# Spills queued later, weight splits ahead of the next group's words, and a group fetched sooner, in a retention and feed-forward kernel

## The chip, the cores and the metric

The kernel runs on one core of one Trainium2 chip. The metric is the device time of one execution in microseconds (us). Smaller is better.

## What is computed

The reference, cut to what matters: a retention attention (B=8, H=8, S=576, D=64), whose output is laid out as 4608 tokens of 512, and a feed-forward layer with h - tanh(h) between two products.

```python
gamma = 1.0 - 2.0 ** (-5.0 - np.arange(H))
Dmat = np.where(rel >= 0, gamma[:, None, None] ** rel, 0.0)   # rel = row - column
ret = (scale * q @ k.transpose(0, 1, 3, 2)) * Dmat @ v
x = ret.transpose(0, 2, 1, 3).reshape(B * S, H * D)           # 4608 x 512
h = x @ w_in                                                  # 512 x 2048
out = (h - np.tanh(h)) @ w_out                                # 2048 x 512
```

## The kernel before

The sequence is cut into nine chunks of 64 positions (NC); one chunk holds 512 tokens (8 batches of 64). Retention runs chunk by chunk with a state, two batches in a turn. [...]

Chunks 0 to 2 go through the feed-forward layer plainly. From chunk 3 on two chunks are taken together, and the products are made with fewer multiplications by sums of quarter blocks (seven products in place of eight). `stage_a` makes the first layer of a pair of chunks, `stage_b` (L1519) the second layer of one chunk, and in its loop over the 16 slices f the attention of the next pair: `attend` (L961) is called for every even f. `stage_b` runs for chunks 2 and 4 with attention. From chunk 5 on there are two calls of `stage_c` (L1251), for chunks 5 and 6 and for chunks 7 and 8. Each has eight passes p, and a pass makes seven products k of the first layer, 0 to 6. The results g go to HBM (`spill`). The second layer of chunks 5 to 8 comes last, as 56 products q of `second_product` (L1458): eight groups (chunk and half) of seven. Each product q needs 8 sets of two matmuls against one of seven weight variants, in the order B11, T1, T2, B22, T3, B21, T4.

The order of the work is written out by hand. `in_order` (L72) ties every engine's instructions to the order in which they are written, SP's DMA issues too. A DMA issue that waits therefore holds all issues behind it on SP, and an instruction that waits on ScalarE or VectorE holds all behind it.

What the change touches:

- `attend` has two branches, for the first and the second chunk of a pair. Both copy the attention's output with ScalarE, put words into the operands of the next products (`put`: high word on ScalarE, low word on VectorE), call `between()`, which is the split of slice f+2 of g (`split`, L1034, a cast on ScalarE at L1042, a low word on VectorE at L1043), and `prep_turn(m + 1, 1)`, which is `scale_v` (L297): four ScalarE instructions (L301), one for each of four heads, on the v of the next turn. In the second branch VectorE forms t3, t1, t2, t4 (L990 to L993) between them, and `put(3, ...)` and `put(2, ...)` need t3 and t1.
- `out_sums` (L1135) forms sums and words of w_out in chunk 4's `stage_b` and elsewhere (VectorE L1153, ScalarE L1156).
- In `stage_c`, `away` (L1287) lets GpSimd subtract the tanh from c22, c12 and c21 (L1288), and SP spills the result (L1289); g11 is made by VectorE and spilled at L1327. In the second call (chunks 7 and 8), `ahead_c` (L1398) is called after each product: it loads weight variants (`load_second`, L1339, at L1351 from `ofull` and at L1354 from `ovar`) by the table `ahead_at` (L1388), splits weights (`split_second`, L1360) and fetches groups (`fetch_group`, L1372). A load waits until the products that read its place are done.
- `fetch_group(k)` fetches the even slices (ge) and the odd slices (go) of group k, 1 MB each (L1385). The second group's are in places that hold weights of `stage_c` (xh0 and xh1).
- `split_second` makes the low word of the weight tile cast in the call before (VectorE L1364), and casts the next tile (ScalarE L1367). Each tile is a quarter of a variant. The last call but one falls on q = 3, the last on q = 4, with the low word of the last quarter of B21.
- `side(q + 3)` makes the words of product q+3: a cast on ScalarE (L1432), a low word on VectorE (L1436), and for the first three products of a group sums of g's quarters (L1434, L1442). The call for a group's first product (slices of ge alone) ends with a sum that needs ge and go. `second_product` copies some results out of PSUM on ScalarE (L1487) and adds others on VectorE (L1492, L1493).

The main loop of the second layer (L1595 on):

```python
for q in range(7 * len(GROUPS)):
    if q + 3 < 7 * len(GROUPS):
        side(q + 3)
    if 0 < q < 5:
        split_second()
    second_product(q)
```

Of the kernel before, what the change touches and what calls it, by code (L numbers as in the profile page):

```python
# [92 lines left out]
def retention_ffn(ctx: ExitStack, tc: tile.TileContext, ins, out, spill, wvar, ovar, ofull):  # L93
    nc = tc.nc
# [636 lines left out]
    for k, (n, f) in enumerate(seq):  # L731
# [12 lines left out]
        elif k in early:  # L744
            p = early[k]
# [160 lines left out]
    def prep_turn(m, t):  # L906
        if m >= len(turns) or (m, t) in prepared:
            return
        if (m, t) == (held, 1) and (m, t) not in came:
            return  # L910
        prepared.add((m, t))
        (scale_q, scale_v)[t](turns[m])
# [12 lines left out]
    def put(v, b, src, sub):  # L925

        hi, lo = [x[:, :, b * C : (b + 2) * C].rearrange("p i (u t) -> p u i t", u=2) for x in xv[v]]
        if sub == 0:
            nc.scalar.copy(hi, src)
        else:  # L930
            nc.vector.tensor_tensor(lo, src, hi.bitcast(F32), op=ALU.subtract)
# [29 lines left out]
    def attend(m, between):  # L961

        j = turns[m]
        c, b = divmod(j, B)
        first, apart = (c - FIRST) % 2 == 0, moved(j)
        if first and b == 0:
            new_xv()
        o, new = stretch(m)
        if first:
            a = pool.tile([P, 2, 4, C], F32, tag="cv", bufs=4, name=f"xa{j}")  # L970
            kept[b] = a
            put(0, b, o[:, :, 0:2], 0)
            put(5, b, o[:, :, 2:4], 0)
            nc.scalar.copy(a, o)
            prep_turn(m + 1, 1)
            between()
            put(0, b, a[:, :, 0:2], 1)
            put(5, b, a[:, :, 2:4], 1)
        else:
            a = kept.pop(b)  # L980
            t13 = pool.tile([P, 2, 2, 2, C], F32, tag="cv", bufs=4, name=f"t13_{j}")
            t24 = pool.tile([P, 2, 2, 2, C], F32, tag="cv", bufs=4, name=f"t24_{j}")
            t1, t3, t2, t4 = t13[:, 0], t13[:, 1], t24[:, 0], t24[:, 1]
            own = pool.tile([P, 2, 4, C], F32, tag="cv", bufs=4, name=f"xb{j}")
            nc.scalar.copy(own[:, :, apart:], o[:, :, apart:])
            if apart:
                nc.scalar.copy(own[:, :, :apart], new[:, :, :apart])
            put(4, b, o[:, :, 2:4], 0)
            prep_turn(m + 1, 1)
            nc.vector.tensor_tensor(t3, own[:, :, 2:4], own[:, :, 0:2], op=ALU.subtract)  # L990
            nc.vector.tensor_tensor(t1, own[:, :, 0:2], a[:, :, 0:2], op=ALU.subtract)
            nc.vector.tensor_tensor(t2, t3, a[:, :, 0:2], op=ALU.add)
            nc.vector.tensor_tensor(t4, a[:, :, 2:4], t2, op=ALU.subtract)  # L993
            put(3, b, t3, 0)
            put(2, b, t1, 0)
            between()
            put(1, b, t2, 0)
            put(6, b, t4, 0)
            put(2, b, t1, 1)
            put(1, b, t2, 1)  # L1000
            put(3, b, t3, 1)
            put(4, b, own[:, :, 2:4], 1)
            put(6, b, t4, 1)
# [238 lines left out]
    def renew(na, v):  # L1242
# [5 lines left out]
        nc.scalar.copy(xh, sources[v])  # L1248
        return lambda: nc.vector.tensor_tensor(xl, sources[v], xh.bitcast(F32), op=ALU.subtract)

    def stage_c(na, m0, lows):  # L1251

        nb, last_ = na + 1, na + 2 == NC
        if not last_:
            new_sources(na)
        for p in range(NPAIR):
            j = NPAIR - 1 - p if last_ else p
            homes_ = (("o0", "own")[p % 2], "new", "h", "h") if last_ else (("o0", "h")[p % 2], "o1", "o2", "o3")
            sums_of = None if last_ else attend_c(m0 + j)
            if sums_of and j == NPAIR - 1:  # L1260
                sums_of()
                sums_of = None
            u2, u4 = [pool.tile([P, BLK], F32, tag=t, name=f"u{t}{na}_{j}") for t in ("gh", "gl")]
            x, y, z, v = [
                psp.tile([P, BLK], F32, tag=t, bufs=2 if t == "h" else 1, name=f"p{w}{na}_{j}")
                for w, t in zip("xyzv", homes_)
            ]
            f1, f2 = 2 * j, 2 * j + 1
            c22, c12 = [pool.tile([P, BLK], F32, tag="g", bufs=3, name=f"c{t}_{na}_{j}") for t in (22, 12)]
            c21 = pool.tile([P, BLK], F32, tag="gl", name=f"c21_{na}_{j}")  # L1270

            def done(k):
                if last_:
                    ahead_c(p, k)
                elif j == NPAIR - 1 and k < 6:
                    lows.append(renew(na, k))

            def low():
                if lows:
                    lows.pop(0)()  # L1280

            def tanh(c):
                th = pool.tile([P, BLK], F32, tag="cv", bufs=4, name=f"th{na}_{j}")
                nc.scalar.activation(th, c, AF.Tanh)  # L1284
                return th

            def away(n, c, f):  # L1287
                nc.gpsimd.tensor_tensor(c, c, tanh(c), op=ALU.subtract)  # L1288
                nc.sync.dma_start(spill[n, f], c)  # L1289

            product_c(na, j, 0, x)
            nc.scalar.copy(u2, x)
            if last_ and p == 0:
                lows.append(renew(na - 2, 6))
            done(0)
            if not last_:
                load_turn(m0 + j + 3, 0)
            product_c(na, j, 1, y)
            nc.vector.tensor_tensor(u2, y, u2, op=ALU.add)
            low()  # L1300
            done(1)
            if not last_:
                load_turn(m0 + j + 2, 1)
                load_raws(6 + j)
            product_c(na, j, 2, z)
            nc.vector.tensor_tensor(u4, z, u2, op=ALU.add)
            if not last_:
                prep_turn(m0 + j + 2, 0)
            if sums_of:
                sums_of()  # L1310
            low()
            done(2)
            product_c(na, j, 3, v)
            nc.vector.tensor_tensor(c22, v, u4, op=ALU.add)  # L1314
            low()
            done(3)
            y = psp.tile([P, BLK], F32, tag=homes_[1], bufs=1, name=f"pw{na}_{j}")
            product_c(na, j, 4, y)
            load_sums(na, j - 2 if last_ else j + 2)
            away(nb, c22, f2)  # L1320
            nc.vector.tensor_tensor(c12, y, u4, op=ALU.add)  # L1321
            done(4)
            product_c(na, j, 5, x, False)
            away(nb, c12, f1)
            g11 = tanh(x)
            nc.vector.tensor_tensor(g11, x, g11, op=ALU.subtract)  # L1326
            nc.sync.dma_start(spill[na, f1], g11)  # L1327
            if not last_:
                prep_turn(m0 + j + 1, 1)
            done(5)  # L1330
            product_c(na, j, 6, v, False)
            nc.vector.tensor_tensor(c21, v, u2, op=ALU.add)
            away(na, c21, f2)
            low()
            done(6)

    second_w = {}

# [30 lines left out]

    group_g = {}  # L1370

    def fetch_group(k):  # L1372

        if k >= len(GROUPS):
            return
        n, h = GROUPS[k]
        group_g[k] = []
        for e in range(2):
            if (k % 2, e) == (0, 0):
                g = const.tile([P, NPAIR, 2 * P], F32, tag="state", name=f"ge{k}")  # L1380
            else:
                tag = {(0, 1): "xl0", (1, 0): "xh0", (1, 1): "xh1"}[k % 2, e]
                g = pool.tile([P, NPAIR, 2 * P], F32, tag=tag, bufs=1, name=f"g{'eo'[e]}{k}")
            src = spill[n].rearrange("(j e) p t -> e p j t", e=2)[e]
            nc.sync.dma_start(g, src[:, :, h * 2 * P : (h + 1) * 2 * P])  # L1385
            group_g[k].append(g)

    ahead_at = {  # L1388
        (0, 0): [(T1, 0), (T1, 1)], (0, 4): [(T1, 2), (T1, 3)], (1, 0): [(B11, 0)], (2, 0): [(B11, 1), (B11, 2)],
# [8 lines left out]
    def ahead_c(p, k):  # L1398

        for at, i in ahead_at.get((p, k), []):  # L1400
            load_second(at, i)
        if (p, k) == (3, 6):
            fetch_group(0)
        if (p, k) == (7, 6):
            fetch_group(1)
            for i in range(4):
                load_second(T4, i)
        if (p, k) in SPLITS:
            split_second()
        if (p, k) in ((5, 5), (6, 2), (7, 0), (7, 2), (7, 3), (7, 4), (7, 5)):  # L1410
            next(pieces)
# [181 lines left out]
    for n in range(LATE, NC, 2):  # L1593
        stage_c(n, 8 * (n - FIRST) // 2 + 8 if n < NC - 2 else None, lows)
    for q in range(7 * len(GROUPS)):  # L1595
        if q + 3 < 7 * len(GROUPS):
            side(q + 3)
        if 0 < q < 5:
            split_second()
        second_product(q)  # L1600
    in_order(tc)


# [71 lines left out]
```

## Time and profile before

| | |
|---|---|
| median of three runs | 845.14 us (844.36 to 847.79) |
| the profiled execution | 844.95 us, of which the span is 843.0 us |
| TensorE busy | 824.9 us, 98% of the span |
| VectorE busy | 598.0 us, 71% |
| ScalarE busy | 409.3 us, 49% |
| GpSimd busy | 97.9 us, 12% |
| mean granted TensorE clock | 0.994 of full speed |
| HBM traffic | 241 GB/s over the span |

The profile is of one execution. PE is TensorE, DVE VectorE, ACT ScalarE, POOL GpSimd, SP the engine that issues nearly all DMAs; a name with a q behind it (SPq) is the engine's queue. L with a number is a line of the kernel. A row of a timeline gives the start in us, the duration, the engine and line, the operation, what is written and read, and in brackets how long the engine was idle before it and what released it. [...]

### The profile page before, as it was taken

Reading aid. Unit: us, or ns where it says so; the run is one execution under the profiler, and the core shown is the slowest. Engines: PE = TensorE matmul, PEld = TensorE weight load, DVE = VectorE, ACT = ScalarE, POOL = GpSimd, SP = SyncE. Lnnn points to the kernel's source line nnn. Section 1 sums busy time; section 2 is a strip of 40 time slices with the busy share of each in tenths; the row PEclk is TensorE's granted clock in tenths of the full one; section 3 lists DMA queues with packets and bytes.
Section 4 is the critical chain, followed back from the end, with each engine's and each line's share of the span. In section 5 each row is a group of like instructions: output and inputs, shape, how many; then the busy total and the mean of one; then the engine's idle time right before and its main releaser. Section 6 shows DMA issues by size and latency. Waiting matters only on the chain. (4 is left out here: it accounts for less than half of the span.)

```text
span 843.0 us, 19242 instructions
## 1 busy us (share of the span) xinstructions
PE 824.9 (98%) x7829; PEld 687.3 (82%) x7830; DVE 598.0 (71%) x947; ACT 409.3 (49%) x772; POOL 97.9 (12%) x79
## 2 busy tenths in 40 slices
PE   7999999999999999999999999999999979999997
PEld 6888888888888888888888788788888868888886
DVE  6999877777567675666657765456855868888884
ACT  4987755544335452423345644244644544454542
POOL 0000001010000001212110003233334410000000
PEclk9999999999999999999999999999999998999999
DMA  9967968885777668576658989785489897444411
GB/s 353 365 239 264 359 212 259 243 264 192 230 274 271 202 238 300 201 279 243 238 149 302 329 298 352 278 292 200 171 290 326 322 323 243 134 126 125 125 32 43
DMA packets 94519, 204.10 MB, mean 242 GB/s; under 512 B 9184, under 2 KB 35168, under 8 KB 90976
## 3 DMA queue, kind: packets, MB, share of 16 engines
q1 hardware_dynamic: 93984, 202.10, 70.3%
q8 instruction: 61, 1.00, 0.5%
q10 hardware_dynamic: 448, 0.79, 0.2%
q14 instruction: 26, 0.21, 0.1%
HBM read 135.22 MB, written 67.63 MB: 241 GB/s over the span
## 5 line engine op out<-in xcount | busy, mean ns | idle before, releaser
L1473 PE MATMUL b<-w,s 128*128 128x512 f32 x336 | 118.9, 401 | 5.3 <-DVE w L1364 4.8
L572 PE MATMUL o<-wo,gh 128*128 128x512 f32 x432 | 111.0, 394 | 1.7 <-issue 1.0
L514 PE MATMUL h<-xh,wi 128*128 128x512 f32 x380 | 96.5, 392 | 0.3 <-ACT wi L148 0.3
L572 PEld LDWEIGHTS o<-wo,gh 128*128 128x128 f32 x432 | 79.8, 188 | 19.8 <-issue 1.2
L1477 PE MATMUL b<-w,s 128*128 128x256 f32 x336 | 87.4, 281 | 0.0
L1288 POOL TENSOR_TENSOR c<-c,th 128x512 f32<-128x512 f32 x48 | 63.7, 1331 | 189.8 <-ACT th L1284 176.9
L514 PEld LDWEIGHTS h<-xh,wi 128*128 128x128 f32 x380 | 70.5, 188 | 15.8 <-ACT wi L148 0.7
L1473 PEld LDWEIGHTS b<-w,s 128*128 128x128 f32 x336 | 62.0, 191 | 17.4 <-DVE w L1364 5.1
L1284 ACT ACTIVATE th<-c 128x512 f32<-128x512 f32 x48 | 30.1, 632 | 83.2 <-DVE c L1314 59.5
L1477 PEld LDWEIGHTS b<-w,s 128*128 128x128 f32 x336 | 64.2, 191 | 3.8
L572 PE MATMUL o<-wo,gl 128*128 128x512 f32 x216 | 59.7, 389 | 0.0
L344 PE MATMUL own<-qk,state 64*64 64x64 f32 x888 | 55.3, 221 | 0.0
L344 PE MATMUL own<-qk,vr 64*64 64x64 f32 x888 | 54.1, 220 | 0.0
L514 PE MATMUL h<-xl,wi 128*128 128x512 f32 x192 | 51.7, 390 | 0.0
L572 PEld LDWEIGHTS o<-wo,gl 128*128 128x128 f32 x216 | 40.5, 188 | 8.5
L344 PEld LDWEIGHTS own<-qk,vr 64*64 64x64 f32 x888 | 44.5, 135 | 0.0
L344 PEld LDWEIGHTS own<-qk,state 64*64 64x64 f32 x888 | 44.5, 134 | 0.0
L1085 POOL TENSOR_TENSOR c<-c,th 128x512 f32<-128x512 f32 x16 | 20.9, 1324 | 192.7 <-ACT th L1081 192.7
L1201 PE MATMUL px<-xhv,raw 128*128 128x512 f32 x128 | 40.8, 398 | 1.8 <-issue 1.8
L514 PEld LDWEIGHTS h<-xl,wi 128*128 128x128 f32 x192 | 36.0, 188 | 7.6
L301 ACT ACTIVATE vr<-vr,vtab 128x128 f32<-128x128 f32 x100 | 32.0, 395 | 11.8 <-DMA vr<-in_qkv_dram 11.8
L344 PEld LDWEIGHTS s<-qk 64*64 64x64 f32 x928 | 29.6, 134 | 9.4 <-issue 5.3
(331 smaller groups left out, 1910.8 us busy)
## 6 DMA issues: line engine op xcount, KB each, us to landing
spill_dram<-c SPq DMA_DIRECT2D x64, 256.0 KB, 3.7
s<-spill_dram SPq DMA_DIRECT2D x62, 256.0 KB, 3.9
qk<-in_qkv_dram SPq DMA_DIRECT2D x29, 512.0 KB, 5.0
vr<-in_qkv_dram SPq DMA_DIRECT2D x29, 512.0 KB, 4.9
wt<-wvar_dram SPq DMA_DIRECT2D x14, 1024.0 KB, 7.5
ws<-wvar_dram SPq DMA_DIRECT2D x13, 1024.0 KB, 5.4
spill_dram<-g SPq DMA_DIRECT2D x36, 256.0 KB, 3.3
rwi<-in_w_in_dram SPq DMA_DIRECT2D x16, 512.0 KB, 6.0
```

What stands on the lines that cost most here:

```text
L301: nc.scalar.activation(v[:, :, i], v[:, :, i], AF.Copy, scale=vtab[:, n, i : i + 1])
L344: nc.tensor.matmul(out_, w, x, start=start, stop=stop)
L514: nc.tensor.matmul(hp, win[f][:, cc // 2, a, cc % 2 * P : (cc % 2 + 1) * P], x[:, cc, :], start=(k == 0), stop=(k == 3 * NCC - 1))
L572: nc.tensor.matmul(ops[n][t], g[:, t * P : (t + 1) * P], wout[f_][:, a, :], start=(f_ == first and k == 0), stop=(f_ == final and k == 2),)
L1085: nc.gpsimd.tensor_tensor(c, c, tanh(c), op=ALU.subtract)
L1201: nc.tensor.matmul(into, w[:, a, k], x[:, k], start=start and i == 0, stop=i == len(terms) - 1, skip_group_check=not start,)
L1284: nc.scalar.activation(th, c, AF.Tanh)
L1288: nc.gpsimd.tensor_tensor(c, c, tanh(c), op=ALU.subtract)
L1473: nc.tensor.matmul(to, hi[:, j], ws, start=fresh and j == 0, stop=last_, skip_group_check=not fresh)
L1477: nc.tensor.matmul(to[:, 0], lo[:, j], ws[:, 0], start=False, stop=False, skip_group_check=not fresh)
```

## The change

Four edits.

1. In `attend`, `prep_turn(m + 1, 1)` is written behind `between()`: v is scaled behind the split of g.
2. In `stage_c`, spills are put on a list and written into SP's order two products later, behind the loads of `ahead_c` at that place; the rest of the list follows at the end of the stage.
3. The second group's go is fetched after product 1 of the last pass and its ge after product 5, in place of both after product 6.
4. In the main loop, `split_second` comes ahead of `side(q + 3)`, and for q = 0 the product comes ahead of `side(3)`.

```diff
@@ attend, first branch
             nc.scalar.copy(a, o)
+            between()
             prep_turn(m + 1, 1)
-            between()
@@ attend, second branch
             put(4, b, o[:, :, 2:4], 0)
-            prep_turn(m + 1, 1)
             nc.vector.tensor_tensor(t3, own[:, :, 2:4], own[:, :, 0:2], op=ALU.subtract)
...
             put(3, b, t3, 0)
             put(2, b, t1, 0)
             between()
+            prep_turn(m + 1, 1)
             put(1, b, t2, 0)
@@ stage_c
+    to_spill = []
+    def spill_made(wait):
+        while to_spill and to_spill[0][0] <= made_at[0] - wait:
+            _, n, f, c = to_spill.pop(0)
+            nc.sync.dma_start(spill[n, f], c)
+    made_at = [0]
...
             def done(k):
+                made_at[0] += 1
                 if last_:
                     ahead_c(p, k)
                 elif j == NPAIR - 1 and k < 6:
                     lows.append(renew(na, k))
+                spill_made(2)
...
                 nc.gpsimd.tensor_tensor(c, c, tanh(c), op=ALU.subtract)
-                nc.sync.dma_start(spill[n, f], c)
+                to_spill.append((made_at[0], n, f, c))
...
-            nc.sync.dma_start(spill[na, f1], g11)
+            to_spill.append((made_at[0], na, f1, g11))
...
             done(6)
+        spill_made(0)
@@ fetch_group, ahead_c
-    def fetch_group(k):
+    def fetch_group(k, parts=(0, 1)):
...
-        for e in range(2):
+        for e in parts:
...
+        if (p, k) == (7, 1):
+            fetch_group(1, (1,))
+        if (p, k) == (7, 5):
+            fetch_group(1, (0,))
         if (p, k) == (7, 6):
-            fetch_group(1)
             for i in range(4):
                 load_second(T4, i)
@@ main loop
     for q in range(7 * len(GROUPS)):
+        if 0 < q < 5:
+            split_second()
+        if q == 0:
+            second_product(q)
         if q + 3 < 7 * len(GROUPS):
             side(q + 3)
-        if 0 < q < 5:
-            split_second()
-        second_product(q)
+        if q:
+            second_product(q)
```

## Rows read from the trace of the kernel before

**Rows 1.** TensorE's waits in the span: us in total, times, longest.
```profile
PE b L1473 <- DVE w L1364: 4.8, 1, 4.8
PE px L1201 <- issue: 1.8, 1, 1.8
PE b L1473 <- ACT u L1487: 0.5, 1, 0.5
```

**Rows 2.** One window of 1 us: busy times by engine, clock, DMA share, GB/s.
```profile
699.00:700.00 1.00, 1.00 (x5) 0.90 (x4) 1.00 (x1) 0.00 (x0) 0.00 (x0) 0.50 1.09 348
```

**Rows 3.** The chain that ended last: start, us, what.
```profile
680.98 12.77 DMA go<-spill_dram
693.78 1.23 DVE sums L1442
```

**Rows 4.** TensorE's timeline: the first matmuls of products 0, 8 and 12.
```profile
673.70 0.39 PE L1473 MATMUL b<-w,s0vr 128*128 128x512 f32 x1
...
703.98 0.39 PE L1473 MATMUL b<-w,s8vr 128*128 128x512 f32 x1
...
715.16 0.39 PE L1473 MATMUL b<-w,s12vr 128*128 128x512 f32 x1
```

**Rows 5.** ScalarE's timeline at the start of the second phase.
```profile
678.41 1.03 ACT L1432 CAST s<-sums 128x1024 fp32r<-128x1024 f32 x1
679.35 0.57 ACT L1487 COPY u<-b 128x512 f32<-128x512 f32 x1
...
681.29 0.59 ACT L1487 COPY p<-b 128x512 f32<-128x512 f32 x1
```

**Rows 6.** VectorE's timeline: a split of w_out and half a total.
```profile
685.95 0.69 DVE L1364 TENSOR_TENSOR w<-w 128x512 fp32r<-128x512 f32 x1
686.55 0.68 DVE L1492 TENSOR_TENSOR t<-b,u 128x512 f32<-128x512 f32 x1
```

**Rows 7.** SP's timeline at the end of the last pass.
```profile
668.77 0.32 SPq L1289 DMA_DIRECT2D spill_dram<-c  x1
...
683.12 6.15 SPq L1354 DMA_DIRECT2D w<-ovar_dram  x4
```

**Rows 8.** Windows of 4 us, with the columns of rows 2.
```profile
670.00:674.00 4.00, 4.00 (x20) 3.30 (x19) 4.00 (x5) 2.19 (x4) 1.49 (x1) 1.00 0.71 227
...
682.00:686.00 4.00, 4.00 (x25) 3.46 (x24) 3.75 (x6) 3.30 (x5) 0.00 (x0) 1.00 0.98 324
686.00:690.00 4.00, 4.00 (x25) 3.50 (x24) 1.66 (x4) 0.00 (x0) 0.00 (x0) 1.00 1.09 370
```

**Rows 9.** DMA issues at 683.1 us: T4's first quarter, KB, us to landing.
```profile
w<-ovar_dram SPq DMA_DIRECT2D x1, 512.0 KB, 11.9
```

**Rows 10.** Timeline in chunk 4's `stage_b`, a turn of the first branch.
```profile
443.20 1.29 ACT L301 ACTIVATE vr<-vr,vtab 128x128 f32<-128x128 f32 x4
...
445.12 0.25 PE L344 MATMUL own<-qk,vr 64*64 64x64 f32 x2
```

**Rows 11.** Timeline there, a turn of the second branch, and TensorE's next wait.
```profile
465.96 1.28 ACT L301 ACTIVATE vr<-vr,vtab 128x128 f32<-128x128 f32 x4
...
468.20 0.74 ACT L929 CAST xhv<-t 128x256 fp32r<-128x256 f32 x2 [0.96 <-DVE t L990]
468.23 0.23 PE L344 MATMUL own<-qk,vr 64*64 64x64 f32 x2
...
468.85 0.61 ACT L1042 CAST gs<-s 128x512 fp32r<-128x512 f32 x1
...
474.87 0.98 PE L572 MATMUL o<-wo,gh 128*128 128x512 f32 x3 [0.65 <-DMA vr<-in_qkv_dram]
```

**Rows 12.** Windows of 1 us, TensorE alone: busy time, clock, DMA share, GB/s.
```profile
527.00:528.00 1.00, 0.00 (x0) 1.00 1.02 385
...
530.00:531.00 1.00, 1.00 (x4) 0.50 0.99 346
...
532.00:533.00 1.00, 1.00 (x4) 0.53 1.01 377
```

## What the change does to the time: a prediction

> **What bounds the kernel now.** I read the page's table of busy times first: TensorE is busy 98% of the span (the table above), so only its idle time and its clock can give anything back. The list of TensorE's waits then names the places: 4.8 us once on VectorE's L1364, 0.5 us on a ScalarE copy at L1487, and 1.8 us on something the profile doesn't show [rows 1]. The first two lie in the second phase (the products q of L1458, from 673 us on). [...] The chain that ended last tells why L1364 was late: the second half of the second group was issued at 680.98 us and took 12.77 us to land, and only then could VectorE do a sum of that group (L1442, 1.23 us) [rows 3]. VectorE works in the written order, and the last low word of w_out is written behind that sum.
>
> **The stall in the second phase.** Its price is read from TensorE's timeline. Product 0 starts at 673.70 us, product 8 at 703.98, product 12 at 715.16 [rows 4]. Four undisturbed products take 11.18 us, 2.795 each; eight would take 22.36 and took 30.28. So 7.9 us are lost in the first eight: 4.8 and 0.5 of waits, and some 2.6 us of the low clock and of starting up. I take all 7.9 as removable and go through what could be late next, with product q starting at 673.70 + 2.795 q.
>
> Product 0 ahead of the words of product 3. ScalarE's copy of product 0 stood behind the cast of those words: the cast at 678.41 us, the copy at 679.35, the copy of product 1 at 681.29 [rows 5]. Changing places, the copy starts at 678.4 and ends at 679.0, before product 2 wants the bank at 679.3: the 0.5 us goes. The cast starts at 678.9, and VectorE's low word for product 3 at 679.95; it ends at 681.2, product 3 starts at 682.1. The copy of product 1 still ends at 681.9, only 0.2 us before product 3 needs its bank; between nothing and 0.3 us may remain, and I take nothing, since the copies keep their sum.
>
> The last low word. Split ahead of the words of q+3, it comes behind the total of product 3 on VectorE: from 679.95 us four low words of s (1.2 us each, as the sum of the same shape [rows 3]), three splits (0.7) and a total (0.7 and a half-width 0.4) [rows 6], and ends at 688.7 us. Product 5 wants it for its last quarter, at 687.7 + 2.1 = 689.8 us. It fits by 1.1 us.
>
> The spills and the second group. SP issues in order and stood behind GpSimd's products: the last spill of the group before at 668.77 us, the second group at 680.98, T4 behind it from 683.12 [rows 3, 7]. The 668.77 us spill still waits for its GpSimd product in the same place, so the change starts there: go at about 669.1, B21's last loads by 671, T3 by 673.4 (two of its homes are read until product 5 of that pass, about 672.4), ge at 673.5, T4 by 676 or as the queue lets it. Behind them come the c spills, and behind those only later fetches. In bytes from 669.1 to T4's end: c 0.26 MB, go 1.05, B21 0.52, T3 2.10, ge 1.05, c 0.26, T4 2.10, together 7.34 MB. At 324 GB/s, what a full queue moved at 682 to 686 us, that is 22.7 us, to 691.8; at 370 GB/s (686 to 690 us) 19.8 us, to 688.9 [rows 8]. Product 6 reads T4's first quarter at 690.5 and its last at 692.6 us; the first quarter lies 1.57 MB ahead, at 684.6 to 687. T3 is there by 681.2 (wanted 684.9), ge by 684.5 (its cast comes at about 685.2). So T4's last quarter has 0.8 to 3.7 us to spare. Before, it landed 11.9 us after its issue [rows 9], later than that, and nobody waited, since TensorE itself was late.
>
> The words of the second group then follow on VectorE by the same durations: low word 7 at 689.9, its sum 691.1, total of product 4, t1, low word 8 at 694.6 (wanted 696.1), its sum, total of product 5, low word 9 at 698.1 (wanted 698.9), low word 10, after its cast of 1.05, at 701.6 (wanted 701.7). These are tight, but instructions of VectorE overlap a little, which I left out. In the stage with the first four groups' spills the deferral moves no load in SP's order, and TensorE waits there only the unnamed 1.8 us; nothing is gained or lost.
>
> **v scaled behind g's split.** This edit moves four ScalarE instructions of each turn (1.28 us together) behind a cast, and in every second turn also behind two casts that wait for VectorE's t3 and t1. I went through all turns: in most, v is still waiting for its load at that point, or TensorE comes 1 us or more later. The closest harmless one is at 443.20 us: a cast (0.52 us) put ahead gives heads at 444.1 to 445.0, and the next attention reads its first v at 445.12 [rows 10]. One turn isn't harmless. There VectorE is behind with the sums of w_out, and t3 comes late. Before, v was scaled from 465.96 us without it, and the attention read its first v at 468.23 [rows 11]. After, ScalarE must first do the casts of t3 and t1 (468.20) and of g (468.85); v's heads come from 469.4 on, the first ready at 469.8, the last at 470.7. TensorE stops for 1.6 us, and then some 0.06 us at each of three heads: 1.8 us. That delay covers the 0.65 us for which TensorE waited, to 474.87 us, on a load issued before the stop [rows 11]; 1.15 us stay. The clock: the nearest row is the unnamed 1.8 us wait at 527 us, beside an attention of the same kind, after which the clock was 0.50 to 0.53 from 530 to 533 us, three windows that lost 1.5 us together [rows 12]. Here a stop of about that length comes just ahead of the attention. The bounds are 0 and 1.5 us; I take 1.5, by that nearest row. What the edit gives (g's words sooner) is nothing, since TensorE never waited for g there.
>
> The sum against the profiled execution's own 844.95 us (0.2 below the median of 845.14): 844.95 - 7.9 + 1.8 - 0.65 + 1.5 = **839.7 us**.
>
> **Rivals.**
> First, v's delay costs less: no clock is lost (838.2), or the stop is covered too (837.0). For it: the stop is somewhat shorter than the wait at 527 us. Against: nothing on ScalarE's written order lets v pass the casts.
>
> Second, something of the second group is late: T4's landing, or VectorE's words 8 to 10. A ring that gives no more than 300 GB/s lands T4 24.5 us after 669.1, at 693.6: a stop of 1 us, and with late words and the clock up to 4. That gives 840.7 to 843.7.
>
> Third, the one that ends slower: T4 is now queued behind both halves of the group. If the queue moves 227 GB/s, as at 670 to 674 us when little was asked of it [rows 8], the 7.34 MB take 32.3 us and T4's last quarter lands at 701.4; TensorE stops in product 6 for 9 us and loses 2 us of clock: 850.7. It is slower than before from where stop and clock exceed 5.3 us, below some 270 GB/s. Against it: both stretches with a full queue [rows 8]. [...]
>
> Fourth, the change doesn't do what it says: go's home is free later than I think, it is issued as late as before, and only the low word moves. Then product 7 waits for its words instead of product 5; some 3 of the 7.9 us are saved: 844.6.
>
> **How the numbers follow.** The forecast, with clock losses from 1 to 2 us (839.2 to 840.2, and 0.6 either way for other executions), has 0.42; the first rival 0.26, the second 0.20, the third 0.07, the fourth 0.05. The range takes in the first rival down to 836.4 and the second up to 843.5. What a measurement can tell from no change is about 0.5%, 4.2 us: faster means below 840.9. That is all of the first rival, 0.34 of the forecast and little of the second: 0.62. Slower is the third, 0.06 of its 0.07. The rest, 0.32, is the same.
>
> **What would show it.** Right: product 8 starts 7.9 us sooner relative to product 0, no wait on L1364, a clock of 1.00 at that place, go issued about 12 us sooner; in the stage with attention a new TensorE wait on L301 of 1.6 to 2 us near 468 us, the 0.65 us gone, a clock of 0.50 for 2 to 3 us behind it. Wrong: TensorE waiting in products 6 to 10 for a load of w or for L1436, no wait on L301, or the unnamed 1.8 us gone or elsewhere, which would move the time by up to 3 us either way.

## The result, and the profile after

Median after: 839.14 us (836.91 to 839.77), against 845.58 (844.36 to 848.54) for the kernel before beside it; the ratio is 0.9914 [0.9892, 0.9936], that is 6.4 us or 0.9% faster. The forecast was 839.7 in a range of 836.4 to 843.5. The time came out; its terms did so only in part, and the runs below show which.

The profiled execution of after took 839.53 us, its span is 837.7 us, TensorE is busy 823.9 us of it and the mean granted clock is 1.00 (0.994 before). The lines have moved: the products' matmuls are now L1489 and L1493, their copies L1503, the casts and low words of g L1448 and L1452, its sums L1458, the split of w_out L1377, the fetch L1398, the loads L1364 and L1367.

TensorE's waits after (as rows 1: us in total, times, longest):

```profile
PE px L1201 <- issue: 2.0, 1, 2.0
PE o L572 <- issue: 1.3, 1, 1.3
...
PE o L572 <- DMA vr<-in_qkv_dram: 0.9, 2, 0.5
PE s L344 <- DVE qk L295: 0.4, 1, 0.4
PE own L344 <- ACT vr L301: 0.4, 1, 0.4
```

The 4.8 us on the low word of w_out (a tile less its cast) [rows 1] is gone and no load has come in its place. The wait on the scaling of v is there (last line); it is the first part of a longer stop, 0.4 us where the prediction had 1.6. The two "issue" waits, which name no cause, were there before too (1.8 and 1.0 us).

The second phase after, TensorE's timeline (as rows 4), one window of 1 us (as rows 2), and SP's timeline (as rows 7):

```profile
675.90 0.39 PE L1489 MATMUL b<-w,s0vr 128*128 128x512 f32 x1
...
698.76 0.40 PE L1489 MATMUL b<-w,s8vr 128*128 128x512 f32 x1
...
709.94 0.40 PE L1489 MATMUL b<-w,s12vr 128*128 128x512 f32 x1
```

```profile
699.00:700.00 1.00, 1.00 (x8) 0.91 (x7) 1.00 (x1) 0.55 (x1) 0.00 (x0) 1.00 0.49 154
```

```profile
671.86 0.43 SPq L1398 DMA_DIRECT2D go<-spill_dram  x1
...
675.78 0.43 SPq L1398 DMA_DIRECT2D ge<-spill_dram  x1
677.36 0.32 SPq L1257 DMA_DIRECT2D spill_dram<-c  x1
678.10 4.36 SPq L1367 DMA_DIRECT2D w<-ovar_dram  x4
```

Products 0 to 7 take 22.86 us in place of the 30.28 of before [rows 4]: 7.42 us gained, 0.5 from the best that was forecast (22.36). The clock at 699 us is 1.00, not 0.50 [rows 2]. go is issued 4.0 us before product 0 starts (671.86 against 675.90), where it used to be issued 7.3 us after (680.98 against 673.70 [rows 3, 4]): 11.3 us sooner. T4's issue begins 2.2 us after the start of product 0 instead of 9.4 [rows 7].

Where the two traces part, as the drift of TensorE's timeline against before (the start of the same attention or product, after minus before). The second execution profiled is the same kernel, run again later (d2 below):

| stretch | after | after, again |
|---|---|---|
| start to 240 us (no edited line runs) | +0.56 | +0.04 |
| 240 to 437 us (chunks 0 to 3) | -0.01 | +0.04 |
| 437 to 512 us (chunk 4 with attention) | +2.46 | -0.25 |
| 512 to 551 us (the unnamed wait and its clock) | -1.31 | +0.20 |
| 551 us to product 0 | +0.50 | +0.15 |
| products 0 to 7 | -7.42 | -7.40 |
| rest | 0.0 | 0.0 |
| sum, the difference of the spans | -5.2 | -7.2 |

So the second phase is the same to 0.02 us, and what differs between two executions of one kernel, 2 us here, lies ahead of it. That is what makes edit 1 hard to price, and seven of the experiments bear on its price.

### The profile page after: what moved, and what is told of

Its sections match the earlier page's. It is cut to its first block, busy times and chain, and to the rows that moved or that the text cites. A ratio compares the mean times of both kernels' runs of the same rounds, so it can differ in the third digit from the quotient of the medians.

```text
span 837.7 us, 19247 instructions
## 1 busy us (share of the span) xinstructions
PE 823.9 (98%) x7830; PEld 685.0 (82%) x7830; DVE 598.6 (71%) x947; ACT 409.7 (49%) x772; POOL 98.0 (12%) x79
## 5 line engine op out<-in xcount | busy, mean ns | idle before, releaser
L1489 PE MATMUL b<-w,s 128*128 128x512 f32 x336 | 117.5, 397 | 0.1
L1493 PE MATMUL b<-w,s 128*128 128x256 f32 x336 | 87.0, 279 | 0.0
L1489 PEld LDWEIGHTS b<-w,s 128*128 128x128 f32 x336 | 61.2, 188 | 12.1 <-ACT u L1503 0.4
L1493 PEld LDWEIGHTS b<-w,s 128*128 128x128 f32 x336 | 63.4, 189 | 3.7
L301 ACT ACTIVATE vr<-vr,vtab 128x128 f32<-128x128 f32 x100 | 31.9, 394 | 7.6 <-DMA vr<-in_qkv_dram 7.6
```

The lines of the kernel that those rows point to most:

```text
L301: nc.scalar.activation(v[:, :, i], v[:, :, i], AF.Copy, scale=vtab[:, n, i : i + 1])
L1489: nc.tensor.matmul(to, hi[:, j], ws, start=fresh and j == 0, stop=last_, skip_group_check=not fresh)
L1493: nc.tensor.matmul(to[:, 0], lo[:, j], ws[:, 0], start=False, stop=False, skip_group_check=not fresh)
```

## The experiments

The table gives for each kernel the median, the ratio to the kernel before, and from its profile the time from product 0 to product 8 and the drift from 437 to 512 us against before. The second to fourth columns hold "old" where an edit is undone.

| kernel | v (edit 1) | spills (2), fetch (3) | order (4) | median us | ratio | products 0 to 7 | 437 to 512 |
|---|---|---|---|---|---|---|---|
| before | old | old, old | old | 845.58 | 1 | 30.28 | 0 |
| after | new | new, new | new | 839.14 | 0.9914 [0.9892, 0.9936] | 22.86 | +2.46 |
| x1 | old | new, new | new | 838.94 | 0.9907 [0.9882, 0.9933] | 22.87 | -1.08 |
| x2 | new | old, old | old | 845.79 | 0.9994 [0.9977, 1.001] | 29.47 | +0.13 |
| x3 | old | old, old | new | 844.64 | 0.997 [0.9952, 0.9988] | 28.85 | +0.52 |
| x4 | old | new, new | old | 838.59 | 0.9907 [0.988, 0.9933] | 23.74 | +0.58 |
| x5 | old | old, new | new | 842.71 | 0.9954 [0.9937, 0.997] | 25.51 | -1.10 |
| x6 | old in one turn | new, new | new | 836.83 | 0.9891 [0.9869, 0.9914] | 22.87 | +0.57 |
| x7 | old | new, old | new | 839.26 | 0.9914 [0.9885, 0.9943] | 24.16 | +2.32 |
| x8 | new in first branch | new, new | new | 838.91 | 0.992 [0.9889, 0.9952] | 22.85 | +0.79 |
| d1 | as x6 | new, new | new | 837.92 | 0.9888 [0.9864, 0.9912] | 22.86 | -0.61 |
| d2 | new | new, new | new | 838.22 | 0.9895 [0.987, 0.9919] | 22.88 | -0.25 |
| d3 | as x1 | new, new | new | 841.1 | 0.9914 [0.9887, 0.9941] | 22.83 | +1.29 |
| d4 | later still in one turn | new, new | new | 839.06 | 0.9904 [0.9878, 0.9931] | 22.63 | +1.03 |

The kernel before had medians of 846.24 beside x1 to x4, 846.1 beside x5 to x8 and 847.4 beside d1 to d4.

### Which edit frees the second phase: x2, x3, x4, x5, x7

**x2, edit 1 alone.** The only edit to the kernel before is the diff of `attend`.

> The kernel before with the move of v behind g's split alone. Theory: 1 to 2.4 us slower than before (845.6): 846.6 to 848.0, with a TensorE wait on L301 near 468 us; the 4.8 us wait on L1364 stays. Rival: no change, 845.6.

Measured 845.79, no change that can be told: the rival's time, not the theory's, though TensorE does wait 0.7 us on L301 (shown with d4 below). The stall of the second phase is all there:

```profile
PE b L1473 <- DVE w L1364: 4.5, 1, 4.5
PE b L1473 <- ACT u L1487: 0.5, 1, 0.5
```

**x3, edit 4 alone.** The kernel before with the new main loop.

> The kernel before with the new order of the main loop alone (splits of w_out and product 0 ahead of the next words). Theory: the wait on L1364 goes, but T4 is issued at 683 us and lands at 695 to 698 as before, and product 6 wants it at 690.5: TensorE waits there for about as long, 4 to 6 us, with the low clock behind it; 842.5 to 844.5. Rival: the order of the words alone was the stall: 838 to 839.

```diff
 for q in range(7 * len(GROUPS)):
+    if 0 < q < 5:
+        split_second()
+    if q == 0:
+        second_product(q)
     if q + 3 < 7 * len(GROUPS):
         side(q + 3)
-    if 0 < q < 5:
-        split_second()
-    second_product(q)
+    if q:
+        second_product(q)
```

Measured 844.64. The wait on the low word, in product 5, is gone, as forecast, and at the start of product 6 TensorE stops for T4, which is still issued late (SP issues go at 683.59 us and T4 from 685.89, 9.5 us after product 0):

```profile
697.28 0.76 PE L1473 MATMUL b<-w,s 128*128 128x512 f32 x1 [3.89 <-DMA w<-ovar_dram]
```

Of the 7.4 us the order alone gives 1.4. A wait was moved, not removed: behind VectorE's stall stood a DMA that was no earlier.

**x4, edits 2 and 3 with the old order.**

> The changed kernel with the old order of the main loop and v as before, so only spills queued later and the second group fetched sooner. Theory: go lands by 684 us, the sum ahead of the last low word is no longer late, and only 1 to 2 us of wait on that word and the 0.5 us on the copy stay: 839.5 to 841.5. Rival: the order of the words is what matters and the 4.8 us stay: 844 to 846.

Measured 838.59, slightly under what was expected. The wait on the low word doesn't come back: with go fetched early, the low word of w_out's last quarter starts at 692.59 us and product 5 wants that quarter at about 693.3. What returns is the copy of product 0 behind the cast of the words of product 3 (TensorE's timeline):

```profile
682.67 0.50 PE L1489 MATMUL b<-w,s 128*128 128x512 f32 x1 [1.05 <-ACT u L1503]
```

So with the spills and the fetch early, edit 4 is worth 23.74 - 22.87 = 0.9 us in the profile, too little for the medians to show.

**x5, the spills at once and the rest of edits 3 and 4.** Beside x1:

```diff
-                to_spill.append((made_at[0], n, f, c))
+                nc.sync.dma_start(spill[n, f], c)
...
-            to_spill.append((made_at[0], na, f1, g11))
+            nc.sync.dma_start(spill[na, f1], g11)
```

> The changed kernel with v as before and with the spills back at once in SP's order: only the sooner fetch of the second group and the new order of the main loop stay. Theory (the queue's bytes decide, and 12 us sooner for go is enough): T3 goes out at about 677 us, ge at 678.5 and T4 at 680.5 to 682; T4's first quarter lands at 688 to 690, about when product 6 wants it, a wait of 0 to 1 us there: 838 to 840.5. Rival (the deferral is what makes the fetch early): T4 lands 3 to 4 us late, 842 to 844.

**x7, the spills late and the fetch in its old place.** Beside x1:

```diff
-        if (p, k) == (7, 1):
-            fetch_group(1, (1,))
-        if (p, k) == (7, 5):
-            fetch_group(1, (0,))
         if (p, k) == (7, 6):
+            fetch_group(1)
             for i in range(4):
                 load_second(T4, i)
```

> The changed kernel with v as before and the second group fetched after product 6 of the last pass, as before: only the later spills and the new order stay. Theory: without the spills ahead of it, ge and go go out at about 675 us in place of 680.5, T4 from 676 to 681, and both land before they are wanted: no wait in products 5 to 8, 838 to 839.5. Rival (the sooner fetch is what counts): T4 still waits behind 2 MB and lands after 692 us: 840.5 to 843.

x5 measured 842.71, the rival's time; x7 839.26, the theory's, though TensorE does wait for T4, which that theory had ruled out. Of the two, putting off the spills is worth more. SP's timelines show why, x5 first, then x7:

```profile
669.86 0.49 SPq L1398 DMA_DIRECT2D go<-spill_dram  x1
...
674.18 2.57 SPq L1301 DMA_DIRECT2D spill_dram<-c  x2
...
679.42 0.58 SPq L1398 DMA_DIRECT2D ge<-spill_dram  x1
680.19 2.83 SPq L1301 DMA_DIRECT2D spill_dram<-c  x1
683.12 2.77 SPq L1367 DMA_DIRECT2D w<-ovar_dram  x4
```

```profile
677.57 0.32 SPq L1257 DMA_DIRECT2D spill_dram<-c  x1
677.94 0.65 SPq L1398 DMA_DIRECT2D ge<-spill_dram  x1
678.64 1.84 SPq L1398 DMA_DIRECT2D go<-spill_dram  x1
680.58 6.13 SPq L1367 DMA_DIRECT2D w<-ovar_dram  x4
```

In x5 go leaves early, but the spills of 674.18 us hold T3 and ge until GpSimd is done, and T4 stands behind one more, which waits for GpSimd until 680.16:

```profile
678.87 1.29 POOL L1300 TENSOR_TENSOR c<-c,th 128x512 f32<-128x512 f32 x1 [2.48 <-issue]
```

The issue of that spill then holds SP for 2.8 us more, for a reason that the profile doesn't show. T4 starts 9.5 us after product 0 (683.12 - 673.62), as late as before. In x7, whose product 0 is at 676.80, T4 starts at +3.8 and go at +1.8. TensorE's waits in the second phase, x5 first, then x7:

```profile
PE b L1493 <- DMA w<-ovar_dram: 0.9, 3, 0.3
PE b L1489 <- DMA w<-ovar_dram: 0.9, 1, 0.9
```

```profile
PE b L1490 <- DMA w<-ovar_dram: 0.6, 2, 0.3
```

Against x1 the first eight products lose 2.6 us in x5 and 1.3 in x7; that is the price of undoing one half. Undoing both (x3) costs 6.0, more than the two together: over x3, putting off the spills alone gives 4.7 us and the sooner fetch alone 3.3. x7's median shows nothing of its 1.3 (839.26, against 838.94 for x1), and x5's median lies 2.7 us over the one execution that was profiled (839.99), so what its longer executions lose, and where, was not seen.

### What scaling v later costs: x1, x6, x8 and d1 to d4

**x1, edit 1 undone.**

> The changed kernel with v scaled where it was before (the first of the four edits undone, the other three kept). Theory: the move of v costs TensorE 0.9 us at one attention near 470 us and lets later loads land late, so that undoing it gives back 1 to 2.4 us against the changed kernel's 839.1: 836.7 to 838.1, and no TensorE wait on L301. Rival: the waits on loads in that stage are chance and v's move costs nothing: 839.1, with the same 2 to 2.5 us lost between 440 and 505 us.

**x6, undone in the one turn that the prediction named.** Beside after:

```diff
             put(4, b, o[:, :, 2:4], 0)
+            if m == held + 3:
+                prep_turn(m + 1, 1)
             nc.vector.tensor_tensor(t3, own[:, :, 2:4], own[:, :, 0:2], op=ALU.subtract)
```

> The changed kernel, but in the one turn of the second branch in which VectorE is behind with the sums of w_out, v is scaled as before. Theory: the attention near 470 us that took 2.9 us takes 2.0 again and there is no wait on L301; but the 0.65 us wait on a load of v some 5 us later comes back, so the time moves by less than 0.5 us: 838.5 to 839.5. Rival (the stop is paid in full, as I forecast): 1.2 us or more faster, 837.9 or less.

**x8, undone in the second branch, kept in the first.**

> The changed kernel with v behind g's split in the first branch of attend alone; in the second branch as before. Theory: no stop at any attention, VectorE's sums of w_out start some 0.6 us sooner against TensorE than in the kernel before, since g's low word isn't held up by the load of v; no loads late at 485 to 505 us; 837 to 839. Rival (the moves cost the same in either branch): as the changed kernel, 839.1, with TensorE 1 us or more late between 485 and 505 us.

None of the three has a wait on the scaling of v. Their medians are 838.94, 836.83 and 838.91: x1 at its rival's time (but with 1.1 us gained from 437 to 512 us, where the rival had 2 to 2.5 lost), x8 within its theory's range (but with a wait of 0.3 us on a load of v at 495 us, which the theory had ruled out). x6 alone stood out, as if the stop were paid in full. Since x6 was timed beside other kernels than after was, x6 and x1 were run once more together with after and with a kernel in which v comes later still:

**d1, d2, d3: x6, after and x1 again.**

> The same kernel as the one with the old place of v in one turn alone, beside the changed kernel on one chip. Theory A (the stop on v's scaling is 0.9 to 1.2 us, and the next wait on a load gives most of it back; the low 836.8 was the spread of executions): its median lies within 1.0 us of that of the changed kernel, 838 to 840. Theory B (the stop is paid in full): it is 1.5 us or more faster than the changed kernel on this chip, about 836.5 to 837.5. Both: no wait of TensorE on the scaling of v.

> The changed kernel once more, as the measure for the other three. Both theories: 838.0 to 840.0, a wait of TensorE on the scaling of v of 0.3 to 0.8 us near 470 us. Theory A lets the waits on the loads of v (0 to 2.5 us in all between 437 and 505 us) differ from the first profile's 0.9; theory B wants them the same.

> Edit 1 undone, beside the changed kernel on one chip. Theory A: within 1.0 us of the changed kernel. Theory B: 1.2 us or more faster than it, and equal to the kernel with one turn undone within 0.7. Both: no wait on the scaling of v.

d1 gave 837.92 and d2 838.22: the 2.3 us between x6 and after shrank to 0.3. d3 gave 841.1, 2.9 above d2, which neither theory had. Its profile (an execution of 841.32) is 2.81 us late already at 240 us, ahead of every edited line, and x1's (837.46, the same kernel) 2.49 us; from 437 to 512 us x1 then gained 1.08 on before, and d3 lost 1.29. Undoing edit 1 gave 0.2 us less in one comparison and 2.9 us more in the other, and both times the intervals of the ratios overlap, so **no price of edit 1 can be read from the times**; it has to be read from the traces.

**d4, v later still.** In the one turn v is scaled behind the casts of t2 and t4 too:

```diff
             between()
-            prep_turn(m + 1, 1)
+            if m != held + 3:
+                prep_turn(m + 1, 1)
             put(1, b, t2, 0)
             put(6, b, t4, 0)
+            if m == held + 3:
+                prep_turn(m + 1, 1)
```

> The changed kernel, but in the one turn with the stop v is scaled behind the casts of t2 and t4 too (0.69 us more of ScalarE). Both: the stop at that attention grows by about 0.7, from 0.9 to some 1.6 us, the length that was forecast. Theory A: the clock stays 1.00 behind it, and the time is 0 to 0.8 us above the changed kernel. The prediction's own step: the clock falls to 0.50 for 2 to 3 us behind a stop of that length, and the time is 1.8 to 2.4 us above the changed kernel.

The stop grew as both had it. TensorE's waits at that attention, x2, after, d4 (d2, the same kernel as after, has none that long, though both theories wanted one):

```profile
470.64 0.27 PE L344 MATMUL own<-qk,vr 64*64 64x64 f32 x2 [0.67 <-ACT vr L301]
```

```profile
470.19 0.27 PE L344 MATMUL own<-qk,vr 64*64 64x64 f32 x2 [0.38 <-ACT vr L301]
```

```profile
471.46 0.27 PE L344 MATMUL own<-qk,vr 64*64 64x64 f32 x2 [0.99 <-ACT vr L301]
```

The listed wait is only its first part: in after the first v is read 0.82 us after the attention's first matmul, against 0.18 in before, and the three heads behind it follow at 0.29 to 0.30 us, against 0.23 to 0.24. The whole stop is what the attention lasts over the 2.02 us that it takes undisturbed: 1.17 us in x2, 0.88 in after, 0.57 in d2, 1.49 in d4. And behind the longest of them the clock stays at 1.00 (a window of d4):

```profile
473.00:477.00 4.00, 4.00 (x55) 3.33 (x46) 3.67 (x7) 1.68 (x5) 0.00 (x0) 1.00 0.99 370
```

So the clock didn't fall behind any of the four stops of 0.57 to 1.49 us, and the step that priced it so has nothing for it here. Each is one execution, though, and the clock behind the unnamed wait near 530 us goes either way (below): that it never falls here isn't shown. d4's median is 0.8 above d2's, the upper end of what was expected without a loss of clock, and within the spread.

## Why the prediction was right or wrong, point by point

**What bounds the kernel: right.** Freed of the late fetch and the late T4, the second phase gave 7.42 us of the 7.9. The 2.6 us that the 7.9 holds for the low clock and for starting up is a difference, not a row. In the trace of before the clock is 0.50 from 693.4 to 700.2 us and TensorE works again from 695.66 on; by the author's estimate 4.5 us at half the clock cost some 2.3. In after it is 1.00 there.

**What could be late next: right in the main, with 0.5 us missed.** Some 0.4 of it is lost at product 2. The prediction took the copy of product 0 to start at 678.4 us, 4.7 us after product 0; it started 5.2 us after, at 681.13. It moved up among ScalarE's instructions, but VectorE came late ahead of it (timelines of VectorE and ScalarE, first before, then after):

```profile
677.16 0.68 DVE L1332 TENSOR_TENSOR c<-pv,ugh 128x512 f32<-128x512 f32 x1
677.87 0.63 ACT L1284 ACTIVATE th<-c 128x512 f32<-128x512 f32 x1 [3.36 <-DVE c L1332]
```

```profile
678.24 1.71 DVE L1458 TENSOR_TENSOR sums<-ge 128x1024 f32<-128x1024 f32 x1
679.88 0.68 DVE L1344 TENSOR_TENSOR c<-pv,ugh 128x512 f32<-128x512 f32 x1
680.59 0.63 ACT L1296 ACTIVATE th<-c 128x512 f32<-128x512 f32 x1 [3.30 <-DVE c L1344]
681.13 0.57 ACT L1503 COPY u<-b 128x512 f32<-128x512 f32 x1
```

The tanh ahead of the copy waits for the last c21 of `stage_c`. That c21 started 3.46 us after product 0 before and 3.98 us after it now, and product 2 starts at 681.75, as the copy ends. The prediction left VectorE's work ahead of product 0 where it had been. The other 0.1 us is lost at product 3, which the copy of product 1 releases; there the prediction allowed for up to 0.3 and took nothing.

What made VectorE late is edit 2, and the prediction has no term for it. In the pass before the last, c12 is written into a place that an earlier c leaves when its spill has landed (VectorE, first before, then after):

```profile
652.20 0.69 DVE L1321 TENSOR_TENSOR c<-pw,ugl 128x512 f32<-128x512 f32 x1
```

```profile
655.06 0.69 DVE L1333 TENSOR_TENSOR c<-pw,ugl 128x512 f32<-128x512 f32 x1 [1.28 <-DMA spill_dram<-c]
```

This wait is 0.56 to 1.90 us in the ten profiles with the spills put off and at most 0.52 in the four with the spills at once. The last c21 follows it: it starts 3.44 to 3.58 us after product 0 where the wait is 0.32 us or none (before, x2, x3), 3.76 to 3.78 where it is 0.52 to 0.56 (x5, d4), and 3.98 to 4.00 where it is 0.85 or more. In those ten TensorE loses 0.01 to 1.17 us between 551 us and product 0, the more the longer the wait (0.50 in after, 0.45 in the mean); in the other four it loses nothing (0.02 at most). So putting off the spills has a price, for which the prediction has no term. Its "nothing is gained or lost" is about the first call of `stage_c`; there SP does put a load (L958) ahead of a spill, but TensorE keeps step with before to 0.05 us.

The last low word ended 15.0 us after product 0, as forecast.

**The loads: right.** go was forecast at 4.6 us ahead of product 0 (669.1 against 673.70) and is issued at 4.0 ahead; ge at 0.2 ahead and 0.1; T4 by 2.3 us behind it, and SP begins it at 2.2. T4's quarters land 11.4 to 12.2 us after their issue, the first at 690.3 us and the last at 694.1; product 6, which starts at 693.16, uses the last from 695.25 on. So T4 had 1.1 us to spare, near the lower end of the 0.8 to 3.7 that the prediction gave it. ge is the miss: it lands 12.7 us after its issue, at 688.5 and so 12.6 us after product 0 started, when 10.8 was forecast. ScalarE waits 0.55 us for it and TensorE not at all. The prediction's sum of bytes lets T4 land behind the fetches issued ahead of it, which is the author's assumption; in this trace the landings kept that order: go landed at 677.3 us, ge at 688.5 and T4's first quarter at 690.3. The queue moved 366 to 409 GB/s from 678 to 690 us, so the slower rival with its 227 GB/s did not come.

**v scaled behind g's split: the place and the mechanism right, the size wrong.** Forecast: a stop of 1.8 us, 0.65 given back, 1.5 of clock, together +2.65. In after's profile the stop is 0.88, what comes back is 0.97, and no clock is lost: together about nothing. That the stop covers the wait on the load, as forecast, is likely but not shown: the wait of 0.65 us is gone in all four profiles with the stop (after, x2, d2, d4), and also in three of the ten without it (x4, x5, x6).

The step that failed is "what the edit gives (g's words sooner) is nothing, since TensorE never waited for g there". TensorE didn't, but VectorE did, and VectorE's lateness was what made the stop. One turn earlier, in the first branch, the cast of g used to stand behind the scaling of v, which waits for its load; g's low word waited with it, and behind the low word the sums of w_out (L1153), behind those t3. ScalarE and VectorE in that turn, before and after:

```profile
458.20 1.28 ACT L301 ACTIVATE vr<-vr,vtab 128x128 f32<-128x128 f32 x4 [2.21 <-DMA vr<-in_qkv_dram]
459.38 1.13 ACT L1042 CAST gh<-s 128x512 fp32r<-128x512 f32 x2
460.02 0.69 DVE L1043 TENSOR_TENSOR gl<-s,gh 128x512 fp32r<-128x512 f32 x1 [3.94 <-ACT gh L1042]
...
461.90 1.29 DVE L1153 TENSOR_TENSOR r<-wo 128x512 f32<-128x512 f32 x2
```

```profile
456.41 0.64 ACT L1042 CAST gh<-s 128x512 fp32r<-128x512 f32 x1
457.08 0.69 DVE L1043 TENSOR_TENSOR gl<-s,gh 128x512 fp32r<-128x512 f32 x1 [0.46 <-ACT gh L1042]
...
462.27 1.29 DVE L1153 TENSOR_TENSOR r<-wo 128x512 f32<-128x512 f32 x2
```

In after one of the two low words is done 3 us sooner. The time is to be read against TensorE's: that turn's attention starts at 460.35 us before and at 461.68 after. Over all fourteen profiles the sums of w_out start 1.34 to 1.87 us behind it where the first branch is old (before, x1, x3, x4, x5, x7, d3), and 0.29 to 1.25 where it is new (after, x2, x6, x8, d1, d2, d4): 1.0 us sooner in the mean, and no overlap. VectorE then begins t3 not 0.30 us ahead of the next attention, as before (ScalarE's cast of it waits until 468.20 [rows 11]), but 1.25 ahead in after, 1.56 in d2 and 0.95 in x2, and the stop is shorter than the forecast by just that: 1.8 - 0.95 = 0.85 in after (measured 0.88), 1.8 - 1.26 = 0.54 in d2 (0.57), 1.8 - 0.65 = 1.15 in x2 (1.17). So the two halves of edit 1 work against each other: its second-branch half makes the stop, and by this sum its first-branch half takes a third to two thirds of it away. No run has the second-branch half alone, so the 1.8 us that the stop would have without the other half is worked out, not measured.

**The clock: wrong as a rule.** It was priced by the unnamed wait of 1.8 us at 527 us [rows 12]. That wait is in every profile, 1.2 to 2.3 us long, and the clock fell behind it in six of the fourteen (before, x3, x4, x7, x8, d2) and not in the others. After and d2 are the same kernel, with waits of 2.03 and 1.93 us. First d2, then after (windows of 1 us behind the wait):

```profile
529.00:530.00 1.00, 1.00 (x4) 0.80 (x3) 0.00 (x0) 0.00 (x0) 0.00 (x0) 0.50 0.93 295
530.00:531.00 1.00, 1.00 (x4) 0.81 (x3) 0.00 (x0) 0.07 (x1) 0.00 (x0) 0.50 1.05 326
```

```profile
532.00:533.00 1.00, 1.00 (x5) 0.82 (x5) 0.00 (x0) 0.00 (x0) 0.00 (x0) 1.00 1.01 221
533.00:534.00 1.00, 1.00 (x6) 0.81 (x5) 0.00 (x0) 0.59 (x1) 0.00 (x0) 1.00 1.00 389
```

What the clock costs there comes and goes from one execution to the next. After gained 1.31 us on before over that stretch (the table of drifts) with a wait 0.27 us longer, so the low clock cost 1.6 us: the size, 1.5, was right for that place, and what failed was to carry it over to the stop. The loss is in the profile of before and not in that of after, so 1.3 of the 5.2 us between these two spans are no merit of the change.

**How the sum came out all the same.** By the sizes measured it should have been 844.95 - 7.42 + 0.88 - 0.97 = 837.4 us, the first rival (837.0 to 838.2). The second profile of after is at 837.52 us. The first, at 839.53, had in addition 0.56 us from before any edited line and new waits from 437 to 512 us: 0.9 us on loads of v, 0.4 on VectorE's L295, 0.3 more at the unnamed wait near 480 us, and what lies around them; and it had the 0.50 ahead of product 0, less the 1.31 of wait and clock near 530. That edit 1 causes the waits from 437 to 512 us isn't shown: the kernels with the old place of v spread from -1.10 to +2.32 us over the same stretch, and x7 has 2.6 us of waits on the loads of v:

```profile
PE o L572 <- DMA vr<-in_qkv_dram: 2.6, 4, 0.9
```

All twelve timed executions of this kernel (after and d2) have a median of 838.6, between the first rival and the forecast. That the time came within 0.6 us of the forecast is luck as far as edit 1 goes: the 2.65 us that the prediction gave it came to about nothing, and delays that it had no term for took their place.

**The other rivals.** The fourth (go not issued sooner) is refuted by SP's timeline, the second and third by the list of waits. The fourth's time was met by x3, where only the order moves (forecast 844.6, measured 844.64), but by another way: the stop is in product 6 on T4, not in product 7 on the words.

**Open.** What TensorE waits for at the two unnamed "issue" waits was not found. Whether undoing edit 1 in the one turn gains anything is open too: d1 and x6 have the lowest medians, 0.3 and 2.3 us under d2 and after. In the profiles the stop of 0.6 to 0.9 us is mostly given back: from that attention to the next the four profiles with v's new place there drift by -0.13 to +0.54 us against before (+0.14 in the mean), the ten with the old place by -0.70 to +0.55 (-0.12). Some 0.3 us in the mean is less than the spread.

## What to carry to other kernels

When an instruction is moved behind another on an engine whose order is written out, follow both directions: who waits longer for what moved back (here TensorE on v, 0.88 us in after), and whose input comes sooner by what moved up, two or three engines on (here the sums of w_out, 1.0 us in the mean), even if the bound engine never waited for that input. A queue whose issues are tied in order, as SP's are here, is best read as a list of what each issue stands behind: here a spill that waited for GpSimd held a weight load that no one would have looked for behind it (T4, issued 9.5 us after product 0 in x5 and 2.2 in after), and taking it out of the way was worth more than the sooner fetch (4.7 us against 3.3, each alone over x3). What is put off can also hold its place in memory longer: here VectorE waited 1.28 us in after for one that came free late, and at most 0.52 us in the four profiles with the spills at once. Before pricing an edit of a microsecond, compare two profiles of one kernel stretch by stretch; a stretch that drifts by 2 us without an edit (437 to 512 us: +2.46 and -0.25 us in two profiles of one kernel) can't confirm or refute such a price, but the length of a single attention, or the time from one product to another, can.

## What the runs showed of the hardware

- The granted clock fell to 0.50 behind the unnamed wait near 530 us in six of fourteen profiles and not in the others: behind 1.93 us in d2, not behind 2.03 us in after, the same kernel. It stayed at 1.00 behind the stops of 0.57 to 1.49 us near 470 us (d2, after, x2, d4). Where it fell near 530 us it cost 1.6 us (before against after).
- Two waits of TensorE that the profile puts down to nothing stand at the same places of the program in profile after profile, a few matmuls behind an attention: near 530 us in all fourteen (1.2 to 2.3 us), near 480 us in ten (0.2 to 1.9 us).
- Ahead of 240 us, where all these kernels are alike, their profiles differ by up to 3.2 us (d1 against before); from there to 437 us they keep together to 0.06 us.
- A spill of 256 KB issued at 646.87 us (after) landed 8.1 us later, with the queue moving 408 GB/s meanwhile, and its place was free for VectorE only then (c12 at 655.06 us, 1.28 us of wait).
